# Turning the attention output of a fifth batch by transposing DMA instead of on TensorE, in a kernel whose instruction order is planned

## The chip, the cores and the metric

The kernel runs on one core of one Trainium2 chip. The metric is the device time of one execution in microseconds (us), the median of several runs. Ratios are computed as the mean time of one kernel's fast runs over the mean of the other's fast runs of the same rounds, so a ratio is not quite the ratio of the medians that stand beside it.

## The reference

The program is linear attention with exponential features, followed by a mixture of eight experts whose routing is normalised eight times over rows and columns (the gate, `P`). Shapes: 8 batches, 8 heads, 576 tokens, 64 channels; the experts see 4608 tokens of 512 features.

```python
def phi(x):
    proj = np.einsum('bhsd,df->bhsf', x, w_phi)
    proj = proj - np.max(np.abs(proj), axis=-1, keepdims=True)
    return np.concatenate([np.exp(proj), np.exp(-proj)], axis=-1)
q_p, k_p = (phi(q), phi(k))
kv  = np.einsum('bhsf,bhsd->bhfd', k_p, v);  z = np.sum(k_p, axis=2)
num = np.einsum('bhsf,bhfd->bhsd', q_p, kv)
den = np.einsum('bhsf,bhf->bhs', q_p, z)[..., None] + 1e-06
attn_out = num / den
# ... rows of attn_out, [4608, 512], are x of the experts:
for e in range(E):
    out += P[:, e:e + 1] * (np.maximum(x @ w1[e], 0.0) @ w2[e])
```

## The kernel before

The kernel is a Python program that collects all operations of the attention part and of the first expert with estimated durations, lets a list scheduler put them in order (`schedule`), and then emits them in that order. Each engine and each DMA queue is given its instructions in order.

```python
    def run(self, tc):
        done = self.schedule()          # sorted by the planner's own durations
        with tc.manual_schedule():
            for o in done:
                o.fn()
```

Queries and keys are loaded by POOL (GpSimd) into a buffer `qk` of which there are two; one half batch (four heads) fills one. SP (SyncE) then turns the whole buffer, 512 KB, with one transposing DMA into `qkT`. SP also loads the values and turns the rest tokens (`rT`).

```python
    ring(a_in, [128, 2, 4, NJ * D], BF16, "qk", 2)
    ring(a_t, [128, 2, 8, 128], BF16, "qkT", 3)
# ...
        for x, src in ((1, k), (0, q)):                       # load_qk
            dma("POOL", nh << 17, 230, lambda x=x, src=src: nc.gpsimd.dma_start(
                out=t["qk"]()[:, x, o:o + nh], in_=src[b, hh:hh + nh, 0:SM]...
# ...
            dma("SP", 1 << 19, 148, lambda: nc.sync.dma_start_transpose(   # turn_qk
                out=t["T"]().rearrange("p a b c -> p (a b) c"),
                in_=t["qk"]().rearrange("p a b c -> p (a b c)")),
                [(t["qk"], *y) for y in rk], [(t["T"], *y) for y in rk])
```

The attention output of a batch (512 main tokens, four pairs of heads) must be turned into `xT`, features on the partitions, before the expert's first matmul can use it. Batches 3 to 6 are turned by DMA; batches 0, 1, 2 and 7 by four TensorE transposes into PSUM (the buffers that TensorE's results go to in this kernel) and a copy on DVE (VectorE) for each pair; ACT is ScalarE:

```python
    def pair_c(b, pr, xb):
        if b in (3, 4, 5, 6,):
            dma("SP", 1 << 17, 148, lambda: nc.sync.dma_start_transpose(
                out=xT[:, pr, b * SM:(b + 1) * SM].rearrange("p (a c) -> p a c", c=128),
                in_=xb()[:, 0:NJ].rearrange("p a b -> p (a b)")), [(xb, 0), (xb, 1)], [("xT", b, pr)])
            return
        pxt = new("P1")
        for j in range(NJ):
            pe(128, lambda j=j: nc.tensor.transpose(
                bf(pxt)[:, j * 128:j * 128 + 128], xb()[:, j, :], ident),
                [(xb, 0), (xb, 1), "ident"], [pxt])
        dve(270, lambda: nc.vector.tensor_copy(
            out=xT[:, pr, b * SM:(b + 1) * SM], in_=bf(pxt)[:, 0:512]),
            [pxt], [("xT", b, pr)])
```

The softmax here doesn't subtract the row's maximum and nothing guards it: scores larger than these inputs give would overflow.

## Time and profile before

| before | value |
|---|---|
| median of 3 runs | 1026.67 us (1026.66 to 1026.98) |
| span of the profiled run, granted clock | 1026.8 us, 0.999 (that execution took 1028.55 us) |
| attention part with the first expert's start | up to about 205 us |
| remaining experts | about 820 us, TensorE 99% busy |

The prediction shows the page's totals and the stretches of the attention part, and explains them. One more view matters later: TensorE, stretch by stretch. The columns are the stretch, its length, then for matmul, weight load, DVE, ACT and POOL the busy us with the number of instructions, then the granted TensorE clock (1.00 is full speed), the DMA share (the queues' shares added, so it can pass 1), and GB/s. In the kernel before:

```profile
core 0: us, PE busy (x) PEld busy (x) DVE busy (x) ACT busy (x) POOL busy (x), PEclk, DMA share, GB/s
75.00:100.00 25.00, 24.74 (x287) 16.68 (x289) 24.06 (x59) 23.70 (x61) 21.32 (x34) 1.00 1.23 189
100.00:125.00 25.00, 24.79 (x276) 16.27 (x279) 22.65 (x51) 24.27 (x61) 18.15 (x28) 1.00 1.25 168
```

TensorE is busy for 49.5 of 50 us at full clock. One caution: the profiled execution took 1028.55 us, more than any of the four timed beside the kernel after (1026.66 to 1027.51). It is late from the start: its second group of gate matmuls (`wgate`) begins at 73.81 us, against 71.3 to 71.9 us in eight of the traces below, of kernels with the same order up to there. So starting times of two traces are not compared as they stand below; I count from that gate or from a neighbouring instruction.

These are the POOL queue's operations around 99 us in the kernel before (start, duration, engine, line, operation; in brackets the idle time before it and what ended it):

```profile
98.84 0.81 POOL L501 DMA_DIRECT2D qk<-in_k_dram  x1 [0.32 <-issue]
99.64 0.76 POOL L501 DMA_DIRECT2D qk<-in_q_dram  x1
100.40 1.94 POOL L761 TENSOR_TENSOR v<-v_m,em 128x1024 bf16<-128x1024 f32 x1
```

### The profile page before, as it was taken

To read this page: it belongs to the slowest core of one execution; us is meant where nothing else is said; L and a number is where in the kernel's file an instruction comes from. 1 tells how busy PE (TensorE), PEld (TensorE's weight loads), DVE (VectorE), ACT (ScalarE), POOL (GpSimd) and SP (SyncE) were. 2 spreads that over 40 slices of the span, in tenths; PEclk is the share of its full clock that TensorE was granted. 3 is DMA by queue.
4 is the path that set the end of the run, shared out by engine and by line. 5 is a ranking of instruction groups with operands and counts; after the bars stand their busy time and mean duration, and the time that the engine had idled before them with its cause. 6 is when DMAs were issued, how large, how long until landed. Compare 5 with 4: busy or idle time off the path is not lost.

```text
span 1026.8 us, 24281 instructions
## 1 busy us (share of the span) xinstructions
PE 1008.1 (98%) x9469; PEld 837.9 (82%) x9504; DVE 823.5 (80%) x1600; ACT 703.9 (69%) x1530; POOL 458.5 (45%) x480
## 2 busy tenths in 40 slices
PE   7899999999999999999999999999999999999998
PEld 4666666645888888888888888888888888888886
DVE  7999989987888887787777877787778877787775
ACT  7999999834888766666666666666665666666663
POOL 5768664400334444444444434544444433444342
PEclk9999999999999999999999999999999999999999
DMA  9999978170232611161115211341116111614333
GB/s 235 192 197 179 177 137 130 37 154 19 85 104 85 124 42 42 47 129 43 48 46 112 54 43 42 75 102 42 42 46 131 42 42 43 130 36 125 133 124 124
DMA packets 112501, 96.03 MB, mean 94 GB/s; under 512 B 54145, under 2 KB 87041, under 8 KB 112385
## 3 DMA queue, kind: packets, MB, share of 16 engines
q1 hardware_dynamic: 80576, 70.55, 26.5%
q0 software_dynamic: 31648, 23.86, 16.6%
q8 instruction: 74, 1.21, 0.5%
q14 instruction: 43, 0.34, 0.1%
q10 hardware_dynamic: 160, 0.07, 0.0%
HBM read 94.98 MB, written 14.16 MB: 106 GB/s over the span
## 4 chain that ended last, share of the span: by engine, by line
PE 93%; ACT 2%; DVE 1%; DMA 1%; SPq 1%; issue 1%; POOL 0%; DVEq 0%; ACTq 0%
PE ps L1273 74%; PE ps L573 17%; PE ps L856 2%; DMA acc<-in_q_dram 1%; ACT q L569 1%; ACT k L569 0%; SPq L495 0%; ACT wx L569 0%; SPq L551 0%; PE ps L885 0%; DMA xd<-S 0%; DVE ps L864 0%; DVE hT L1305 0%; DVE m L565 0%; POOL wx L761 0%
## 5 line engine op out<-in xcount | busy, mean ns | idle before, releaser
L1428 POOL TENSOR_TENSOR acc<-acc,V 128x512 f32<-128x512 f32 x248 | 314.8, 1280 | 484.5 <-ACT V L1425 426.7
L1301 ACT COPY U<-ps 128x512 f32<-128x512 f32 x378 | 217.0, 586 | 166.2 <-PE ps L1273 150.9
L1305 DVE CUSTOM_DVE_ANT_0 hT<-ps,U 128x512 bf16<-128x512 f32 x378 | 254.6, 687 | 87.7 <-PE ps L1273 59.9
L1425 ACT ACTIVATE V<-ps,P 128x256 f32<-128x256 f32 x496 | 208.1, 473 | 90.7 <-PE ps L1273 82.1
L1413 DVE SCALAR_TENSOR_TENSOR acc<-ps,P,acc 128x256 f32<-128x256 f32 x372 | 159.1, 478 | 69.5 <-PE ps L1273 69.2
L1273 PEld LDWEIGHTS <-S 128*128 128x128 bf16 x1984 | 194.1, 98 | 22.6 <-issue 0.2
L1273 PEld LDWEIGHTS <-T 128*128 128x128 bf16 x1512 | 148.0, 98 | 17.2
L1273 PEld LDWEIGHTS <-hT 128*128 128x128 bf16 x1488 | 145.6, 98 | 16.8
L1273 PE MATMUL ps<-X,T 128*128 128x256 bf16 x1008 | 152.4, 273 | 0.0
L1273 PE MATMUL ps<-T,S 128*128 128x256 bf16 x1056 | 135.8, 273 | 0.0
L1273 PEld LDWEIGHTS <-wx 128*128 128x128 bf16 x1152 | 112.7, 98 | 13.6 <-issue 0.2
L1181 DVE TENSOR_TENSOR S<-hT 128x1024 bf16<-128x1024 bf16 x124 | 87.2, 712 | 10.1 <-ACT hT L1310 9.9
L1273 PEld LDWEIGHTS <-w 128*128 128x128 bf16 x864 | 84.5, 98 | 9.8
L1273 PE MATMUL ps<-xT,wx 128*128 128x256 bf16 x576 | 88.4, 273 | 0.1
L1273 PE MATMUL ps<-X,wx 128*128 128x256 bf16 x576 | 86.8, 273 | 0.0
L1310 ACT ACTIVATE hT<-ps 128x512 bf16<-128x512 f32 x126 | 73.2, 606 | 9.8 <-PE ps L1273 9.8
L1273 PE MATMUL ps<-wx,hT 128*128 128x256 bf16 x560 | 77.6, 273 | 0.0
L1273 PE MATMUL ps<-xT,T 128*128 128x256 bf16 x504 | 76.7, 273 | 0.0
L573 PE MATMUL ps<-xT,w 128*128 128x512 bf16 x270 | 70.5, 379 | 0.7
L573 PE MATMUL ps<-w,hT 128*128 128x512 bf16 x276 | 69.8, 379 | 0.7 <-ACT q L569 0.2
L1273 PE MATMUL ps<-T,hT 128*128 128x256 bf16 x496 | 69.2, 273 | 0.0
L1273 PE MATMUL ps<-xT,w 128*128 128x256 bf16 x432 | 66.5, 273 | 0.0
(129 smaller groups left out, 1426.5 us busy)
## 6 DMA issues: line engine op xcount, KB each, us to landing
X<-xd SPq DMA_DIRECT2D x126, 256.0 KB, 2.7
wx<-in_moe_w_dram POOLq DMA_DIRECT2D x8, 1024.0 KB, 12.4
v_m<-in_v_dram SPq DMA_DIRECT2D x15, 512.0 KB, 5.6
out_dram<-acc SPq DMA_DIRECT2D x14, 512.0 KB, 2.9
w<-in_moe_w_dram POOLq DMA_DIRECT2D x6, 1024.0 KB, 12.1
xd<-S SPq DMA_DIRECT2D x18, 256.0 KB, 2.1
qk<-in_k_dram POOLq DMA_DIRECT2D x12, 256.0 KB, 5.5
qk<-in_q_dram POOLq DMA_DIRECT2D x12, 256.0 KB, 6.4
```

The lines of the kernel that those rows point to most:

```text
L569: act(el, lambda: nc.scalar.activation(out=dst(), in_=src(), func=ACT.Exp, bias=0.0, scale=scale), r, w)
L573: nc.tensor.matmul(out_, lhsT=lhsT, rhs=rhs, start=start, stop=stop)
L856: pe(65, lambda j=j: nc.tensor.matmul(pn()[:, j * D1:j * D1 + D1], lhsT=s["T"][x]()[:, j % 2, 2 * h + j // 2, :] if j < 4 else r["T"][x]() ...
L1181: lambda: f.tensor_tensor(out=out_(), in0=x(), in1=y(), op=op), r, w, **kw)
L1273: pe(256, lambda i=i, k=k, z=z: nc.tensor.matmul(bank()[:, 256 * i:256 * i + 256], lhsT=lhs(k, i), rhs=rhs(k), start=first and z, stop=k = ...
L1301: act(512, lambda: nc.scalar.copy(out=u[fp][n]().rearrange("p a b -> p (a b)"), in_=x[fp]()), [x[fp]], [u[fp][n]])
L1305: dve(515, lambda: nc.vector._custom_dve(ADD_SAT, out=out_(fp, i, j), in0=bank[fp]().rearrange("p (a b) -> p a b", a=2), in1=u[fp][n](), s ...
L1310: act(512, lambda: nc.scalar.activation(out=out_(fp, i, j), in_=x[fp]().rearrange("p (a b) -> p a b", a=2), func=ACT.Relu, bias=0.0, scale ...
L1413: dve(320, lambda n=n, ts=ts: nc.vector.scalar_tensor_tensor(out=acc[g][:, ts, 256 * j:256 * j + 256], in0=bank()[:, 256 * n:256 * n + 256 ...
L1425: act(370, lambda n=n: nc.scalar.activation(out=u()[:, n, :], in_=bank()[:, 256 * n:256 * n + 256], func=ACT.Copy, bias=0.0, scale=P[:, 4 ...
L1428: pool(695, lambda: nc.gpsimd.tensor_tensor(out=acc[g][:, 2 * i:2 * i + 2, 256 * j:256 * j + 256], in0=acc[g][:, 2 * i:2 * i + 2, 256 * j: ...
```

## The change

The intent is to take batch 2 off TensorE, DVE and PSUM as well, so that five batches instead of four are turned by DMA. The list of steps is the same; the planner sorts anew.

```diff
     def pair_c(b, pr, xb):
-        if b in (3, 4, 5, 6,):
+        if b in (2, 3, 4, 5, 6,):
             dma("SP", 1 << 17, 148, lambda: nc.sync.dma_start_transpose(
```

## The prediction

> **What bounds the kernel now.** I read the page first: busy time, and the chain that ended last.
>
> ```profile
> PE 1008.1 (98%) x9469; PEld 837.9 (82%) x9504; DVE 823.5 (80%) x1600; ACT 703.9 (69%) x1530; POOL 458.5 (45%) x480
> PE 93%; ACT 2%; DVE 1%; DMA 1%; SPq 1%; issue 1%; POOL 0%; DVEq 0%; ACTq 0%
> ```
>
> TensorE is the resource of the whole program, and 93% of the chain is TensorE work. The expert part (from about 205 us on) is not touched by the change; a microsecond won or lost before 205 us should reach the end unchanged. So the question is what the change does to the attention part. The view of stretches of time comes next (columns: stretch, length, busy us with instruction counts of matmul, weight load, DVE, ACT, POOL; granted clock; DMA share; GB/s).
>
> ```profile
> 30.00:75.00 45.00, 40.97 (x526) 29.22 (x530) 43.35 (x103) 43.45 (x107) 33.01 (x54) 1.00 1.18 182
> 75.00:205.00 130.00, 128.78 (x1493) 85.00 (x1513) 118.93 (x279) 122.78 (x301) 82.92 (x133) 1.00 0.87 134
> ```
>
> From 75 to 205 us TensorE shows 99%, ACT 94%, DVE 91%: three engines look full at once. But these busy times hold each instruction's latency, which overlaps with the next one's start. So I took start-to-start times from the timeline: a 128x512 exponential shows 0.67 us but seven in a row take 3.51 us, so one occupies (3.51 - 0.67)/6 = 0.47; a DVE maximum shows 0.68 but the next starts 0.60 later; eight 512-column matmuls take 1.89 us, so (1.89 - 0.38)/7 = 0.216 each; sixteen 65-column ones take 0.68, so 0.032 each. With the counts of the groups by form for the first 210 us:
> TensorE: 364 expert matmuls x 0.216 = 79, some 1150 of 65 columns x 0.032 = 37, 288 of 256 columns x 0.11 = 32, 72 projections of 512 columns x 0.216 = 16, everything else about 19; sum 183 us.
> ACT: 256 exponentials and 64 expert evictions x 0.47 = 150, 24 more of that size 11, 32 half-size 9, about 90 tiny ones 10; sum 180 us.
> DVE: 144 maxima x 0.60 = 86, 128 normalisations x 0.40 = 51, 64 reciprocals x 0.10 = 6, 32 kv copies x 0.34 = 11, copies into xT 10, the rest 12; sum 176 us.
> These are estimates from the trace, and they say the attention part is balanced: three engines with about 180 us of work each in 205 us, the difference being the start (inputs arriving) and many small waits. No single engine is a wall, so taking work from one buys less than that work.
>
> **What the Trainium skill says.** "Perfetto Trace Analysis", section Identifying the Most-Contended Engine, says that matmul busy share is a poor measure because pipelined matmuls mislead. The trace agrees: 99% busy, yet my count leaves some 10% of hidden gaps. "TensorE: Matmul & The Clock Gate", Part 4: PE-mode transpose: the result of such a transpose lands in PSUM, so a DVE copy must follow, and one takes about 275 ns in a kernel. Here one is 218 ns long and four together 0.39, and the copy does follow. "DMA: Bandwidth & Descriptors", section Latency and other measured facts, gives a transposing DMA 261 GB/s in its strided case: 128 KB would move in 0.50 us (an estimate from that figure). The trace shows much more from issue to landing, because of latency and queueing:
>
> ```profile
> L879 SPq DMA_TRANSPOSE xT<-xb x10: 1190/1194/1403, 96.0 to 189.9; - x10
> L879 SPq DMA_TRANSPOSE xT<-wx x6: 1189/1193/1935, 100.4 to 165.3; - x6
> DMA to landing us min/median/max: 2.3/4.2/7.7
> ```
>
> Those are the 16 turns of batches 3 to 6 that already go by DMA: 1.2 us of the SP queue each, 2.3 to 7.7 us to land. The same page, Rules for kernel authors, asks that transposes of two streams be serialized; all here are on the SP queue, so the change adds no such wait.
>
> **The change, part by part.** Batch 2 has four head pairs. The timeline shows their present turns: TensorE at 73.6, 78.5, 86.2 and 90.3 us.
>
> ```profile
> 86.24 0.39 PE L885 MATMUL ps<-ident,xb 128*128 128x128 bf16 x4
> 90.28 0.39 PE L885 MATMUL ps<-ident,xb 128*128 128x128 bf16 x4
> 88.19 0.39 DVE L888 COPY xT<-ps 128x512 bf16<-128x512 bf16 x1
> 91.01 0.42 DVE L888 COPY xT<-ps 128x512 bf16<-128x512 bf16 x1
> 96.31 1.89 PE L573 MATMUL ps<-xT,w 128*128 128x512 bf16 x8
> ```
>
> Removed: 16 TensorE transposes in groups of four. The next matmul starts 0.23 us after a group's start (73.58 to 73.81), so 4 x 0.23 = 0.9 us of TensorE. Removed too: four DVE copies of some 0.42, which hold DVE about 0.35 us (63.26 to 63.60), together 1.4 us. And four uses of a PSUM bank (of eight), each from transpose to end of copy: 1.0 us for the first (73.58 to 74.62), 2.3 us for the third (86.24 to 88.58). ACT loses nothing.
> Added: four 128 KB transposing DMAs, 4 x 1.2 = 4.8 us of the SP queue and perhaps 2 us of the DMA engines (4 x 0.5, estimate above).
> Moved: the Python planner sorts every instruction anew from its own durations, so the order on all engines shifts from about 73 us on, although the list of steps is the same. Nothing in the profile prices that.
> Is the DMA in time? The last pair's normalised output is ready at 89.56 us (89.08 + 0.48), and the first expert matmuls that use batch 2 (the 96.31 row; they follow the 64 of batches 0 and 1) reach that pair's part at about 97.0. That leaves 7.4 us for a turn with a median of 4.2 and a worst of 7.7, plus the time it queues on SP. The SP queue there:
>
> ```profile
> 84.84 1.36 SPq L518 DMA_TRANSPOSE qkT<-qk  x1
> 86.50 5.42 SPq L637 DMA_TRANSPOSE rT<-qk_r  x2
> 92.09 1.84 SPq L518 DMA_TRANSPOSE qkT<-qk  x1
> 94.06 1.00 SPq L509 DMA_DIRECT2D v_m<-in_v_dram  x1
> 95.97 1.20 SPq L879 DMA_TRANSPOSE xT<-xb  x1
> ```
>
> It is nearly solid from 84.8 to 97 us. The first two turns (ready at 73.3 and 78.0) find free places between 76 and 84 us; the last two either go ahead of the two rT turns and push everything behind by 2.4 us, or wait behind them. The data of the rT turns is first used at 103.5, so that is harmless; the query and key turn at 92.09 and the v load slip by 2.4 us, into the idle queue after 97.2.
> Sum if all is hidden: at most 0.9 (TensorE) to 1.4 (DVE) us. As ACT, just as full, is not relieved, I count half: -0.6 us. Against it I set +1.5 us for lost order: the step string and the set of batches look tuned together, and a re-sorted plan around a tuned one is more often worse. That 1.5 is judgement, some 1% of the 130 us after the change. 1026.7 - 0.6 + 1.5 = 1027.6 us.
>
> **The rivals.** (1) Clean gain: the turns hide and the freed slots on TensorE and DVE are used: 1025.3 to 1026.2. For it: both engines are nearly full in 75 to 205, and no wait of TensorE on a DMA of over 0.2 us lies between 70 and 130. Against: ACT. (2) DMA becomes the bound in this stretch: between 80 and 95 us the DMA share is 1.25 to 1.47 (the two queues overlap), so the turns or the loads behind them land late and TensorE starves: 3 to 6 us, 1030 to 1033. For it: landings up to 8.2 us for the query and key turns already. Against: each of those is issued many us ahead, and the planner fills a known delay with other work. (3) Only the order moves: gaps appear or vanish by a us or three with no relation to batch 2: 1024 to 1030. (4) The SP queue is in order, so a turn waiting for a late DVE result blocks the v and key loads behind it; this adds 1 to 3 us, 1028 to 1030.
>
> **Range and chances.** Rival 1 gives the lower end, 2 the upper: 1025.2 to 1031.5 holds them 8 times in 10. Two per cent is 20.5 us, a tenth of the attention part; the removed work is a twentieth of that, and to lose so much TensorE would have to stand still for several landings of the worst size. Faster by over 2%: 0.005; within 2%: 0.98; slower: 0.015.
>
> **What would show it.** Right: 16 fewer TensorE transposes (48 left) and four fewer DVE copies into xT (12 left), 20 DMA turns of xT, TensorE busy down by about 1 us or less, the expert part of the same length to 0.3 us, and the end of attention (last gate, now at 205.6 us) moved by the same amount as the total. ACT's work stays equal. Wrong: a wait of TensorE of over 1 us on an xT or qkT DMA between 90 and 105 us means rival 2; waits at SP's turns with late loads behind them, rival 4; a gain of over 1.5 us means that the banks or the new order gave more than the removed work; a difference in the expert part would contradict the first paragraph.

## More of the kernel before

POOL issues two loads of batch 5 into the second `qk` buffer and then scales the values of a half batch (`v`), which TensorE multiplies with the keys' features without a wait:

```profile
102.58 0.68 PE L573 MATMUL ps<-v,k 128*128 128x65 bf16 x16
```

Neither load waits for a turn here.

"Before" was run again beside every group of kernels, and each kernel is compared with the runs of before that it shared a chip with.

## The result and the profile after

| | before | after |
|---|---|---|
| median (range), 4 runs each, same chip | 1026.83 us (1026.66 to 1027.51) | 1036.38 us (1035.24 to 1037.79) |
| ratio of the means of the fast runs | | 1.0092 (95%: 1.0075 to 1.0110) |
| span of the profiled run, granted clock | 1026.8 us, 0.999 | 1035.6 us, 0.996 |
| start of the last gate's matmuls | 204.83 us | 213.54 us |

The change costs 9.5 us, about 0.9%: within 2%, but outside the predicted range. The last gate starts 8.7 us later and the span is 8.8 us longer, so all of it is lost in the attention part. (The trace of before is itself a slow execution, as said above; counted from the second gate to the last, before takes 131.02 us and after 141.86, 10.8 us more.) The page of the kernel after has 16 matmuls and four DVE instructions fewer, as predicted, but TensorE's busy time is up by 2.7 us (1010.8 against 1008.1), and there is a new entry, the query and key turn, in the chain that ended last:

```profile
PE 1010.8 (98%) x9453; PEld 838.4 (81%) x9488; DVE 822.9 (79%) x1596; ACT 704.6 (68%) x1530; POOL 459.0 (44%) x480
...
PE ps L1273 73%; PE ps L573 16%; PE ps L856 1%; DMA qkT<-qk 1%; DMA acc<-in_q_dram 1%; DVE m L565 1%; POOL v L761 0%; ACT q L569 0%; ACT k L569 0%; DVE ps L864 0%; DVE wx L565 0%; PE ps L703 0%; DVE xb L870 0%; DMA xd<-S 0%; ACT kr L569 0%
```

The stretches tell where. In the kernel after, first in 25 us, then two in 5 us (columns as above):

```profile
75.00:100.00 25.00, 22.20 (x244) 14.26 (x248) 21.23 (x51) 21.71 (x55) 18.88 (x30) 1.00 1.39 169
100.00:125.00 25.00, 19.76 (x187) 12.63 (x187) 16.26 (x37) 16.98 (x42) 13.94 (x21) 0.86 0.95 136
...
105.00:110.00 5.00, 3.15 (x51) 2.89 (x51) 1.82 (x5) 0.90 (x3) 4.64 (x6) 0.57 0.85 164
110.00:115.00 5.00, 4.78 (x35) 2.71 (x34) 4.07 (x10) 3.46 (x10) 0.42 (x3) 0.75 1.07 179
```

TensorE is busy 2.5 us less in the first stretch and 5.0 us less in the second, and in the second its clock is below full speed. The later stretches, 125 to 200 us, are nearly as full as before (73.9 of 75 us against 74.3). TensorE's timeline of the kernel after shows both standstills as bracketed waits:

```profile
97.16 1.24 PE L573 MATMUL ps<-xT,w 128*128 128x512 bf16 x5 [2.54 <-DMA xT<-xb]
...
106.85 1.04 PE L573 MATMUL ps<-v,k 128*128 128x65 bf16 x16 [4.96 <-POOL v L767]
```

The first is the wait for the last of the four new turns. The second, twice as long, is a wait for the scaled values from POOL, an operation that has nothing to do with batch 2. Why POOL was late is in POOL's own timeline of the kernel after:

```profile
103.86 0.80 POOL L501 DMA_DIRECT2D qk<-in_k_dram  x1 [6.28 <-DMA qkT<-qk]
104.69 1.92 POOL L761 TENSOR_TENSOR v<-v_m,em 128x1024 bf16<-128x1024 f32 x1
```

The load of the second half of batch 5 may not overwrite its `qk` buffer before the turn that reads that buffer has landed. POOL stands 6.28 us in front of that load, and the value product is behind it in the same queue. The turn in question is the sixth of the query and key turns (second half of batch 4); I call it **the sixth turn**. It is the one that the prediction showed at 92.09 us. The SP queue of the kernel after, where "x2" counts instructions of a group:

```profile
83.11 5.06 SPq L518 DMA_TRANSPOSE qkT<-qk  x1
88.26 1.51 SPq L879 DMA_TRANSPOSE xT<-xb  x1
89.95 3.10 SPq L637 DMA_TRANSPOSE rT<-qk_r  x2
93.16 1.21 SPq L879 DMA_TRANSPOSE xT<-xb  x1
94.97 3.33 SPq L518 DMA_TRANSPOSE qkT<-qk  x1
98.41 0.52 SPq L509 DMA_DIRECT2D v_m<-in_v_dram  x1
```

Two of the new turns (88.26 and 93.16) stand between the fifth query and key turn (83.11) and the sixth, and hold the queue for 1.51 + 1.21 = 2.7 us. The fifth turn itself holds it for 5.06 us, where it was 1.36 in before (84.84, shown in the prediction); the two `rT` turns hold it 2.3 us less. Counted from the start of the fifth turn, the sixth starts after 11.86 us, against 7.25 in before: it slips by 4.6 us. It also lands 8.3 us after its issue instead of 4.3, by the same view of the two traces. The chain of waits of the kernel after (start, duration, what) makes the link from there to TensorE:

```profile
93.16 1.82 DMA xT<-xb
94.97 8.33 DMA qkT<-qk
...
104.69 1.34 POOL v L761
...
106.85 1.04 PE ps L573 x16
```

**The sum.** Standstills: 2.5 + 5.0 us. Clock: the matmuls from 106.85 to 112.13 us, which last 5.28 us in the kernel after, take 2.92 us when the start-to-start times of the same groups are added up in the kernel before: 2.4 us. Together 9.9, of the 10.8 us by which the stretch from the second gate to the last grew. For the rest e2, described below, gives an estimate: with the new order and without any turn of batch 2 that stretch takes 132.75 us, 1.7 more than in before, of which 1.0 is a wait for POOL's product at the place of the 5.0; the other 0.7 makes the sum 10.6. The sum is an account of one trace against one trace. The Trainium skill, "TensorE: Matmul & The Clock Gate", Part 1: The HAM clock gate, says that TensorE's clock falls to half after an idle window of about 3.4 us and comes back after about as long a busy stretch. The trace agrees: after the standstill of 5 us the clock in 105 to 110 us is 0.57, and it is full again in 115 to 120 us. Other standstills here do not follow it (closing list).

This is a reading of a few traces. Whether the sixth turn is the cause, and what makes it late, was left to experiments.

### The profile page after: what moved, and what is told of

Read it like the earlier page. It is cut to its first block, busy times and chain, and to the rows that moved or that the text cites. A ratio compares the mean times of both kernels' runs of the same rounds, so it can differ in the third digit from the quotient of the medians.

```text
span 1035.6 us, 24246 instructions
## 1 busy us (share of the span) xinstructions
PE 1010.8 (98%) x9453; PEld 838.4 (81%) x9488; DVE 822.9 (79%) x1596; ACT 704.6 (68%) x1530; POOL 459.0 (44%) x480
## 3 DMA queue, kind: packets, MB, share of 16 engines
q8 instruction: 74, 1.21, 0.5%
HBM read 94.98 MB, written 14.16 MB: 105 GB/s over the span
## 4 chain that ended last, share of the span: by engine, by line
PE 92%; DVE 2%; DMA 2%; ACT 2%; issue 1%; POOL 1%; SPq 0%; DVEq 0%; POOLq 0%; ACTq 0%
PE ps L1273 73%; PE ps L573 16%; PE ps L856 1%; DMA qkT<-qk 1%; DMA acc<-in_q_dram 1%; DVE m L565 1%; POOL v L761 0%; ACT q L569 0%; ACT k L569 0%; DVE ps L864 0%; DVE wx L565 0%; PE ps L703 0%; DVE xb L870 0%; DMA xd<-S 0%; ACT kr L569 0%
```

## The experiments

My theory was that the added transposing DMAs take time of the SP queue, so that the sixth turn and the last new turn come late, and POOL's in-order queue hands the delay on to TensorE. The rivals were: the planner's new order alone costs the time; the bytes of the added DMAs cost it; TensorE's direct wait for the new turns' data costs it; the place of POOL's load in its queue is the weak point and moving it cures it. Line numbers differ by some 5 to 20 between the kernels, as lines were inserted. In the edits shown, `# ...` marks lines left out; assertions are left out too.

| kernel | this, median us (range) | before, same rounds | ratio (95%) |
|---|---|---|---|
| e1 old order, four DMA turns | 1036.77 (1035.56 to 1037.33) | 1026.40 | 1.0098 (1.0083 to 1.0113) |
| e2 new order, no turns | 1028.62 (1028.19 to 1029.07) | 1026.40 | 1.0021 (1.0004 to 1.0037) |
| e3 after, POOL load moved | 1034.31 (1033.20 to 1035.16) | 1026.40 | 1.0075 (1.0060 to 1.0090) |
| e4 old order, pairs 0 and 1 | 1029.07 (1026.09 to 1032.37) | 1026.40 | 1.0026 (1.0003 to 1.0049) |
| e5 old order, pairs 2 and 3 | 1032.95 (1029.78 to 1034.23) | 1027.21 | 1.0052 (1.0033 to 1.0071) |
| e6 before + four idle turns | 1035.87 (1031.85 to 1040.11) | 1027.21 | 1.0085 (1.0054 to 1.0116) |
| e7 before + four idle copies | 1028.11 (1027.08 to 1028.74) | 1027.21 | 1.0008 (0.9991 to 1.0024) |
| e8 before + four quarter turns | 1033.61 (1028.88 to 1035.59) | 1027.21 | 1.0056 (1.0027 to 1.0085) |
| e10 e6, loads held | 1031.60 (1030.97 to 1032.40) | 1026.91 | 1.0044 (1.0029 to 1.0059) |
| e11 after, loads held | 1039.02 (1037.40 to 1042.30) | 1026.91 | 1.0119 (1.0098 to 1.0141) |
| e12 before, loads earlier | 1026.74 (1026.06 to 1027.35) | 1026.91 | 0.9996 (0.9981 to 1.0011) |
| e13 e1, loads held | 1032.63 (1030.15 to 1037.87) | 1026.91 | 1.0070 (1.0040 to 1.0100) |
| e16 before, sixth turn late | 1037.11 (1036.54 to 1037.47) | 1026.21 | 1.0103 (1.0087 to 1.0120) |
| e17 e16, loads held | 1034.92 (1034.65 to 1035.84) | 1026.21 | 1.0083 (1.0067 to 1.0098) |
| e15 after, loads behind the product | 1036.04 (1033.41 to 1037.98) | 1026.21 | 1.0090 (1.0069 to 1.0111) |
| e9 batches 4 to 6 only | 1028.67 (1028.17 to 1029.59) | 1026.21 | 1.0021 (1.0006 to 1.0036) |

Four runs each of the kernels. e4, e6, e8 and e13 spread over 6 to 8 us from run to run, where before, in the rounds of the result, spreads over 0.9 us, and a trace shows one run: those of e4, e5, e6 and e11 are the slowest of their four, that of e13 is the fastest. So for these the trace tells which waits occur, and the table what they cost.

### e1 and e2: the turns without the new order, and the new order without the turns

e1 keeps the planner's input, and so the order of before, and puts a transposing DMA where the DVE copy of batch 2 was; the transposes are not emitted.

```diff
+        by_dma = b == 2 and pr in (0, 1, 2, 3)
         for j in range(NJ):
-            pe(128, lambda j=j: nc.tensor.transpose(
+            pe(128, (lambda: None) if by_dma else lambda j=j: nc.tensor.transpose(
# ...
-        dve(270, lambda: nc.vector.tensor_copy(
+        dve(270, (lambda: nc.sync.dma_start_transpose(
+            out=xT[:, pr, b * SM:(b + 1) * SM].rearrange("p (a c) -> p a c", c=128),
+            in_=xb()[:, 0:NJ].rearrange("p a b -> p (a b)"))) if by_dma else
+            lambda: nc.vector.tensor_copy(
```

> Planned exactly as the kernel before, so every engine keeps its old order; only the 16 transposes and 4 copies of batch 2 are left out and a transposing DMA is issued on the SP queue where each copy stood. Theory (late DMAs: the turns on a full SP queue land late, and hold up the query and key turns and, through them, the in-order POOL queue): still slower than before by 2 to 8 us, with a wait of TensorE on the xT DMA near 97 us and a wait of a POOL load on the qkT turn near 99 us. Rival (the re-sorted order is what costs): 1026 us or a little less, since the old order is kept and TensorE has 0.9 us less to do.

e2 keeps the order of after and emits nothing for batch 2's turns; that part of `xT` is set to zero at the start. Its result is wrong (relative error 0.35).

```diff
-            dma("SP", 1 << 17, 148, lambda: nc.sync.dma_start_transpose(
+            dma("SP", 1 << 17, 148, (lambda: None) if b == 2 else lambda: nc.sync.dma_start_transpose(
# ...
+                      nc.vector.memset(xT[:, :, 2 * SM:3 * SM], 0.0)), w=["wphi2"])
```

> Planned exactly as the kernel after, but the four turns of batch 2 are not issued at all; the batch 2 part of xT is set to zero at the start (wrong result on purpose). Theory (late DMAs): the loss is gone, 1024 to 1028 us, POOL waits less than 2 us for the qkT turns. Rival (re-sorted order): stays at 1033 to 1037 us, as every engine has the order of the kernel after.

Measured: the turns in the old order cost 10.4 us, the new order without them 2.2 us. The two don't add up to the 9.5 us of the change, and need not, as one wait can hide another. The order is not the cause: the four DMAs without it cost all of the time, and without the DMAs the new order costs 2 us (expected were 1024 to 1028). In e1 the biggest wait of TensorE is another one than in after, though. Its timeline has

```profile
103.86 2.29 PE L573 MATMUL ps<-xT,w 128*128 128x512 bf16 x5 [8.19 <-DMA xT<-xb]
```

because there the last new turn stands behind the sixth turn in the SP queue (issued at 96.87 after 94.21), while POOL waits 6.40 us on the sixth turn too. Two waits lie side by side, and the longer one sets the time.

### e4 and e5: two pairs at a time

Both are e1 with fewer pairs.

```diff
-        by_dma = b == 2 and pr in (0, 1, 2, 3)     # e1
+        by_dma = b == 2 and pr in (0, 1)           # e4;  (2, 3) in e5
```

> As the first run of this call, but only pairs 0 and 1 of batch 2 go by DMA (their turns fall at 74 and 78 us, where the SP queue has free places); pairs 2 and 3 stay on TensorE. Theory (late DMAs on a full SP queue): 1025.5 to 1027.5 us, no new wait. Rival (any additional transposing DMA in a stretch in which the DMA engines are full costs): slower than before by 1 to 4 us.

> The old order, pairs 2 and 3 of batch 2 by DMA, pairs 0 and 1 on TensorE. Theory: most of the loss of all four is here, since these two fall among the four large turns of 84 to 94 us and the last one is needed 7 us after it is ready: 1031 to 1036 us, with a wait of TensorE of over 3 us on an xT DMA. Rival (loss grows with the number of turns, wherever they are): about as slow as pairs 0 and 1, 1028 to 1030 us.

Measured: 2.7 us for the first two pairs and 5.7 us for the last two, 8.4 together against 10.4 for all four. e4 missed its expectation of no new wait: TensorE waits 2.38 us for POOL's value product (in its slowest run; its fastest, 1026.09, lost nothing). No added turn stands between the fifth and the sixth turn there, yet the sixth starts 9.46 us after the fifth (93.81 against 84.35), 2.2 later than in before. What has changed is the fifth turn:

```profile
84.35 5.29 SPq L518 DMA_TRANSPOSE qkT<-qk  x1
```

It holds the queue for 4.05 to 5.53 us in all eleven kernels with two DMAs added some 3 to 13 us ahead of it, plain copies too, and for 1.35 to 1.36 in the seven others, e5 among them; the two `rT` turns behind it then take 2.5 to 3.8 us instead of 5.4 to 6.3. Why is not known. In e5 the sixth turn is as late (91.75, 9.47 us after the fifth), but it lands in 4.3 us, as in before, where e4's takes 6.1; POOL doesn't wait, and TensorE waits 5.00 us for the data of the last new turn. So there are two ways to lose: the sixth turn lands too late for POOL, or the last new turn lands too late for TensorE.

### e6, e7 and e8: what of a DMA costs, when nobody waits for its data

These keep before whole and add DMAs behind batch 2's DVE copies, into the part of `xT` of batch 7, which is written properly much later. Nobody reads what they write.

```diff
+        def copy():
+            nc.vector.tensor_copy(out=xT[:, pr, b * SM:(b + 1) * SM], in_=bf(pxt)[:, 0:512])
+            if b == 2:
+                nc.sync.dma_start_transpose(                        # e6: four turns of 128 KB
+                out=xT[:, pr, 7 * SM:8 * SM].rearrange("p (a c) -> p a c", c=128),
+                in_=xb()[:, 0:NJ].rearrange("p a b -> p (a b)"))
# e7: nc.sync.dma_start(out=... the same ..., in_=xb()[:, 0:NJ]), four plain copies of 128 KB
# e8: nc.sync.dma_start_transpose(out=xT[:, pr, 7 * SM:7 * SM + 128], in_=xb()[:, 0]), four turns of 32 KB
```

> The kernel before with its order and all its TensorE turns of batch 2, plus four more transposing DMAs of 128 KB at the same four places of the SP queue; they write a part of xT that is overwritten much later, so nothing waits for their result. Theory (the additional turns delay the other DMAs: the qkT turns land later, the POOL loads that wait for them block the v product, and TensorE stands): slower than before by 3 to 7 us although no one needs the added data; the wait of a POOL load on a qkT turn of 2.5 us or more shows. Rival (the loss is the direct wait of TensorE on the late xT turns, 8.2 us in the first run): 1026 to 1027.5 us.

> The same as the run with four idle turns, but the four additional DMAs are plain copies of the same 128 KB from SBUF to SBUF. If what costs is the bytes on the full DMA engines, as slow as the idle turns within 1.5 us. If it is the transposing (a turn holds the SP queue or the engines longer than its bytes), at least 2 us faster than with the idle turns, 1026 to 1028 us.

> The same as the run with four idle turns, but each turn moves a quarter, 32 KB. If the cost is DMA engine time in proportion to the size, a quarter of the loss of the idle turns, up to 1.5 us over before; if it is a fixed price of each issue on the SP queue, about the whole loss.

Measured: idle turns cost 8.7 us, quarter turns 6.4 us, and plain copies of as many bytes as the full turns 0.9 us, which isn't told from nothing (the interval holds 1). So neither the bytes nor the wait for the data explains the loss; of the DMAs added, only the transposing ones made it. The SP queue shows one difference between them. In e7 and e8, the third of the four:

```profile
91.14 0.51 SPq L892 DMA_DIRECT2D xT<-xb  x1
```

```profile
92.32 1.15 SPq L892 DMA_TRANSPOSE xT<-xb  x1
```

A plain copy holds the queue 0.48 to 0.58 us, a turn 1.12 to 1.23 even with a quarter of the bytes. In e7 the sixth turn starts at 91.82, lands in 4.6 us, and POOL waits 0.56 us; in e8 it starts at 93.65 and lands in 10.3 us. Counted from the fifth turn's start, that is 7.54 and 9.43 us, 1.9 us apart: 0.6 by the longer hold of the added turn (1.15 against 0.51), and 1.2 by that of the fifth turn (5.29 against 4.05). POOL's timeline of e8 has the same picture as after's, and the value product follows at 106.06:

```profile
104.50 0.81 POOL L501 DMA_DIRECT2D qk<-in_k_dram  x1 [8.27 <-DMA qkT<-qk]
```

The Trainium skill, "DMA: Bandwidth & Descriptors", Issuing engines are not separate DMA queues, says two things that bear on this: that the time to initiate a DMA on its engine is usually small relative to the DMA itself, and that DMAs of all issuing engines run on the same 16 DMA engines and interleave. On the first e8 agrees: a turn's issue took 1.12 to 1.23 us, its landing 5.2 in the median. Yet four of them cost 6.4 us, so a small issue time is no small cost where the queue is full. That the time in the queue, and not the work in the DMA engines, is the price is argued, not tested apart; what speaks for it is that from 0 to 205 us the packets of the hardware queue, SP's, take 57.9% of the DMA engines' time in e8 and 59.2% in e7 (57.2% in before). On the second see e10 to e17.

### e16: the sixth turn late, and nothing else

The sharpest test adds no DMA at all. It is before with the sixth turn moved two places later in the SP queue, behind the v load and one turn of `xT`, which move up in exchange.

```diff
     def run(self, tc):
         done = self.schedule()
+        turn = self.turns[5]
+        at = done.index(turn)
+        to = [i for i in range(at + 1, len(done)) if done[i].eng == "SP"][1]
+        done.insert(to, done.pop(at))
# ... turns: a list to which turn_qk appends each whole turn
```

> The kernel before, nothing added; the sixth qkT turn stands two places later on the SP queue, behind the v load and the first xT turn of batch 3, so it starts near 97 us instead of 92, after the POOL loads of 95.5. Theory (race): it lands in 8 to 11 us instead of 4.3, a POOL load waits 5 us or more for it, TensorE waits for the v product, and the time is 1030 to 1036 us without a single added transfer. Rival (it takes added turns): it lands in 4 to 6 us and the time stays under 1029 us.

Measured: +10.9 us, with the same instructions as before. The turn starts at 96.41 and lands in 8.1 us. POOL's and then TensorE's timeline of e16:

```profile
105.06 0.81 POOL L507 DMA_DIRECT2D qk<-in_k_dram  x1 [7.48 <-DMA qkT<-qk]
```

```profile
108.79 1.04 PE L580 MATMUL ps<-v,k 128*128 128x65 bf16 x16 [7.04 <-POOL v L774]
```

Counted from the fifth turn, the sixth starts after 11.76 us, against 7.25 in before and 11.86 in after. A sixth turn that is 4.5 us late is enough to lose as much as the change does, through the chain that the trace of after shows. This settles the main point: the slip of this one turn, which the prediction called harmless, costs. It doesn't show that the slip is all that costs in after: there TensorE also waits for the last new turn, and e5 loses 5.7 us by that wait with its sixth turn landed in time.

### e3 and e15: the load taken out of the product's way

If the value product suffers only because a waiting load stands ahead of it in POOL's queue, moving that load should help. e3 is after with the k load of batch 5's second half moved behind the next product and its cast; e15 moves all four loads of batch 5 behind the product.

```diff
# e3, on after
+        at = done.index(self.later)               # the k load of batch 5, heads 4 to 7
+        to = [i for i in range(at + 1, len(done)) if done[i].eng == "POOL"][1]
+        done.insert(to, done.pop(at))
# e15, on after; held: the four q and k loads of batch 5, stop: the last non-DMA POOL
# operation ahead of the last of them
+        for o in self.held:
+            done.remove(o)
+        at = done.index(stop) + 1
+        done[at:at] = self.held
```

> The kernel after with one change on POOL: the load of k for the second half of batch 5, which waits 6.3 us for the landing of a qkT turn, is issued after the v product that stands behind it, instead of ahead. Theory (the POOL queue is blocked by that load, and TensorE waits 5.0 us for the v product and then runs at a cold clock): 5 to 8 us faster than after, 1028 to 1031 us, and no clock dip at 105 to 115 us; the 2.5 us wait on the xT DMA stays. Rival (DMA bandwidth is simply short, the block on POOL is only where it shows): the wait reappears elsewhere and the time stays within 2 us of after, 1034 to 1037 us.

> The kernel after, with all four POOL loads of batch 5 (q and k, both halves) behind the v product of that place, so that no v product stands behind a load that waits for the sixth qkT turn. Theory: the 5.0 us wait of TensorE for the v product and most of the cold clock go; the wait on the late xT turn (2 us) and the late key and query data stay: 1029 to 1032 us. Rival (the DMA engines are simply overloaded): 1034 us or more, TensorE then waiting for other late data.

Measured: 7.9 us over before for e3 and 9.8 for e15, against 9.5 for the change; both missed their theory (1028 to 1031 and 1029 to 1032 us), and the rivals' ranges hold them. The 5 us wait is gone from both traces, and the time is hardly better. In e3 POOL then waits 3.27 us on the same turn one operation later, and TensorE 2.91 us at 106.52 for an ACT result. In e15 TensorE's timeline shows two standstills in other places:

```profile
98.26 2.29 PE L586 MATMUL ps<-xT,w 128*128 128x512 bf16 x5 [2.63 <-DMA xT<-xb]
...
124.68 1.01 PE L586 MATMUL ps<-wphi,qkT 128*128 128x256 bf16 x6 [2.73 <-ACT wx L582]
125.48 3.42 PE L586 MATMUL ps<-w,hT 128*128 128x512 bf16 x8
```

The first is after's wait for the last new turn. The second goes back to POOL again: at 118.05 a k load had waited 3.05 us for a result of TensorE, and a product and a scaling were behind it, for which ACT waited 2.90 us. Each standstill is followed by slow matmuls: the five at 98.26 take 0.42 us each from start to start, where after's five at 97.16 take 0.21. From 75 to 125 us TensorE is busy 5.4 us less than in before, and the clock of 0.96, 0.97 and 0.93 in three stretches of 25 us stands for another 3.5 us (25 x 0.14), an estimate that together makes 8.9; from the second gate to the last, e15 takes 9.8 us longer than before (140.85 against 131.02). So the load in front of the product is the way by which the delay of the turn came to TensorE in after, but not the only way: once the loads are late, the delay comes by the next one. The rival, that moving the load cures it, falls.

### e10, e11, e12, e13 and e17: does the turn land late because it meets loads?

In after the sixth turn starts 4.6 us late and takes 4.0 us longer to land. If transfers of both queues interleave, as the page cited under e8 says, the theory follows: in before the turn has a lead over POOL's loads of batch 5's first half (92.09 against 95.49) and runs mostly alone; in after it starts when the k load at 93.30 is already in flight. e10, e11, e13 and e17 are e6, after, e1 and e16 with these two loads held back by three POOL operations; e12 is before with them earlier.

```diff
# e10 on e6, e11 on after, e13 on e1, e17 on e16; held: the k and q loads of batch 5, heads 0 to 3
+        last = max(done.index(o) for o in self.held)
+        to = [i for i in range(last + 1, len(done)) if done[i].eng == "POOL"][2]
+        stop = done[to]
+        for o in self.held:
+            done.remove(o)
+        at = done.index(stop) + 1
+        done[at:at] = self.held
# e12 on before: the same two loads put ahead of the second POOL operation before them
+        to = [i for i in range(first) if done[i].eng == "POOL"][-2]
```

> The run with four idle turns (1035.9 us), and the two POOL loads of q and k for the first half of batch 5 issued three POOL instructions later. In the runs so far the second large qkT turn of this stretch lands in 4.3 to 4.6 us where it is issued 1.5 us or more ahead of these loads, in 6.1 at 0.8 to 1.0 ahead, and in 8.2 to 10.3 level with them or behind. Theory (a race: additional turns make this turn late on the SP queue, so that it meets the loads in the DMA engines): with the loads held back the turn lands in 4 to 5.5 us although the four turns are still there, the POOL wait on it falls below 3 us, and the time to 1027 to 1030 us. Rival (the number of turns itself slows everything, the loads don't matter): the turn still takes over 7 us and the time stays above 1033 us.

> The kernel after with the same two loads held back. Theory: the turn of 95 us lands in 4 to 5.5 us instead of 8.3, the 5.0 us wait of TensorE for the v product and the cold clock that follows are gone, and the xT wait shrinks to 1 us or so: 1027 to 1030 us. Rival: over 1033 us.

> The kernel before, without any added turn, but the same two loads issued ahead of the v product that stood before them on POOL, so some 2 us earlier, about 1 us after the qkT turn starts instead of 3.4. Theory: the turn lands in 6 us or more instead of 4.3, the POOL load behind it waits 1 to 3 us, and TensorE loses 1 to 5 us: 1028 to 1032 us. Rival (it takes the additional turns): 1026 to 1027.5 us.

> The first run (old order, all four turns by DMA, 1036.8 us), with the two loads held back. Theory: the last xT turn, which stands behind the qkT turn on the SP queue and landed 8.2 us late, lands 3 to 5 us earlier, since the turn ahead of it is not slowed: 1029 to 1033 us. If it reached 1026 the change would pay nothing and cost nothing.

> As the run with the late turn, and the two loads of the first half of batch 5 three POOL instructions later, at about 98.5 us. Theory: with 1.3 us or so of lead the equally late turn lands in 4.3 to 6.5 us, the POOL wait is 3 to 5 us shorter than in that run, and the time at least 2 us less. Rival: no difference over 1 us.

What the traces show of the sixth turn in the kernels, with its lead over the first of these loads (negative where the load was first):

| kernel | turn starts | load starts | lead | lands after |
|---|---|---|---|---|
| before | 92.09 | 95.49 | 3.4 | 4.3 us |
| e9 | 90.20 | 93.54 | 3.3 | 4.3 us |
| e15 | 97.72 | 103.35 | 5.6 | 4.6 us |
| e13 | 93.03 | 96.63 | 3.6 | 4.8 us |
| e10 | 94.75 | 96.53 | 1.8 | 5.4 us |
| e5 | 91.75 | 93.41 | 1.7 | 4.3 us |
| e7 | 91.82 | 93.34 | 1.5 | 4.6 us |
| e17 | 94.98 | 96.40 | 1.4 | 7.6 us |
| e12 | 89.59 | 90.95 | 1.4 | 4.3 us |
| e2 | 90.44 | 91.45 | 1.0 | 6.1 us |
| e4 | 93.81 | 94.63 | 0.8 | 6.1 us |
| e1 | 94.21 | 94.31 | 0.1 | 8.2 us |
| e11 | 97.73 | 97.52 | -0.2 | 11.0 us |
| e8 | 93.65 | 93.19 | -0.5 | 10.3 us |
| e6 | 98.13 | 97.52 | -0.6 | 10.3 us |
| e3 | 94.64 | 93.88 | -0.8 | 8.7 us |
| after | 94.97 | 93.30 | -1.7 | 8.3 us |
| e16 | 96.41 | 94.55 | -1.9 | 8.1 us |

No run shows the interleaving itself, only the landings. With a lead of 1.4 us or more the turn lands in 4.3 to 5.4 us, with 0.8 to 1.0 in 6.1, with less in 8.1 to 11.0, in all kernels but e17. In time, holding the loads went both ways. e10 is 4.7 us above before where e6 was 8.7, and e13 5.7 where e1 was 10.4; in e13's trace, its fastest run, POOL's wait no longer reaches TensorE, which keeps one wait of 3.44 us, on the last new turn. In e10 the turn is about as late as in e6 (9.62 us after the fifth turn's start, against 9.97) and lands in 5.4 us instead of 10.3, so there the gain goes with the lead; the time, 1031.6, still misses the 1027 to 1030 expected. e11 was a miss: it is worse than after (12.1 us above before); in its trace the sixth turn slid to 97.73, and the held load stood just ahead of it all the same. e12 did what it was to do, and its theory failed: the lead fell from 3.4 to 1.4 us, the landing stayed at 4.3, and the time didn't change (-0.2 us). e17 has the same lead of 1.4 us, yet its turn takes 7.6 us, and the kernel is only 2.2 us better than e16. So the lead is not the whole cause. In e17 (as in e16) the v load of 512 KB was issued ahead of the turn, at 91.38; it may be the traffic that the turn met there. That is argued, not tested.

### e9: one batch fewer

If turns by DMA are dear in this queue, fewer of them might be better than before.

```diff
-        if b in (3, 4, 5, 6,):
+        if b in (4, 5, 6,):
```

> Replanned with only batches 4, 5 and 6 by DMA; batch 3, whose turns fall at 96 to 114 us, goes back to TensorE. Theory: four fewer turns in a stretch where they cost, against 0.9 us of TensorE and 1.4 us of DVE more: 1024 to 1028 us, the re-sorted order being worth 2 us either way (the run without any turns of batch 2 was 1.6 to 2.2 us slower than before). Rival (turns are worth what they relieve): 1028 us or more.

Measured: 2.5 us slower than before. Whether turning batch 3 on TensorE is what costs isn't shown: the planner sorted anew here too, and in e2 a new order alone was 2.2 us. No version tried is told apart from before on the faster side.

## Why the prediction was wrong

**What held.** There are 16 fewer matmul records and four fewer DVE instructions, 20 DMA turns of `xT`, ACT's work is equal, and the last gate moved by 8.7 us with the span's 8.8: the expert part is untouched. TensorE's busy time did not fall as said; it rose by 2.7 us, as matmuls at half clock are busy for longer (the sixteen behind the 5 us standstill 1.04 us, in before 0.68). "+1.5 us for lost order" was about right: e2 measures 2.2 us for the new order without the turns, which also holds whatever the planner gains by it. That this came out near is partly luck: the prediction called it judgement. Two of the signs that the prediction named for its rivals appeared: a wait of TensorE of over 1 us on an `xT` DMA between 90 and 105 us (2.54 us), and late loads behind the turns in the SP queue (the v load comes 15.3 us after the fifth turn's start, in before 9.2).

**The step that failed.** The prediction wrote: "The data of the rT turns is first used at 103.5, so that is harmless; the query and key turn at 92.09 and the v load slip by 2.4 us, into the idle queue after 97.2." The slip was foreseen, at 2.4 us; counted from the fifth turn it was 4.6, as the fifth turn too held the queue longer (5.06 us against 1.36). With it falls the step before, that the first two turns "find free places": e4, with these two alone, made the sixth turn 2.2 us late. But the mistake that matters is "harmless". For the `rT` turns the prediction asked when their *output* is first used, for the sixth turn only whether the queue has room. The turn also *frees* a buffer: there are two `qk` buffers, and POOL's next k load waits for the turn to have read one of them. That load stood at 98.84 in before, 2.4 us after the turn had landed (92.09 + 4.3 = 96.4). So the slack was 2.4 us, and behind the load in the same queue was a product that TensorE needed at 102.58. A slip of 4.6 and a landing 4.0 longer, less 2.4 of slack, leave 6.2 us; POOL waited 6.28. e16 shows that such a slip, with nothing added, costs 10.9 us.

**The landing.** The prediction took the landing times of before as they were. The sixth turn's went from 4.3 to 8.3 us when it slipped, nearly as much again as the slip. A lead over POOL's loads goes with it in 17 of 18 kernels; e17 is the exception, and e12 with the same lead of 1.4 us lands in 4.3, so what doubles it stays open.

**The wait on the new turns' own data.** The prediction left 7.4 us for a last turn with a median landing of 4.2 and counted it as hidden. The last new turn was issued at 93.16 behind the two `rT` turns, and TensorE waited 2.54 us for it. e5 and e1, where it was 5.00 and 8.19 us, show that this is a loss in its own right when the turn falls behind the sixth.

**The rivals' sizes.** Rival 4 was the right mechanism in part ("The SP queue is in order"), but it saw the block in the loads behind the turn on SP, where the costly one was POOL's; it was sized at 1 to 3 us, and rival 2 at 3 to 6. Neither counted the half clock after a long standstill (2.4 us here), nor that two standstills add up. The loss in the trace is made of 2.5 + 5.0 + 2.4 us and some 0.7 of new order.

**The balance of the engines.** The prediction set 99% busy, which is 75 to 205 us, against a count of 183 us, which is the first 210, start included (196 us busy by the profile), and found some 10% of hidden gaps and no wall. Redone with its own times for 75 to 205 us alone, the count is about 125 of 130 us (an estimate): some 4% of gaps. TensorE is close to a wall there, so little of a standstill can be made up.

**Copies against turns.** The prediction priced a turn at 1.2 us of the SP queue; e8 shows 1.12 to 1.23, the trace after 1.21 to 1.60. It had no price for what the turns do to the fifth turn's hold. Copies with half the issue time and the same bytes cost 0.9 us, which is not told from nothing.

## What to carry to other kernels

When an added instruction delays another in an in-order queue, don't ask only when the delayed one's result is first read; ask also which buffer it sets free, which load waits for that buffer, and what stands behind that load in its own queue. A delay of 4.5 us in a DMA queue came out as 10.9 us in e16, as it picked up a longer landing and, after the standstill, a slower TensorE clock. To test a suspect, delay it alone in the kernel before, with nothing added: if that gives a loss of the size in question, the suspect is enough for it. The rest of the change isn't acquitted by that; e5 shows a second way to lose. And before two traces are subtracted, check that each is a typical run, and count from a common point.

## What the Trainium skill lacked or had wrong

- "DMA: Bandwidth & Descriptors" gives a transposing DMA as a bandwidth and, in its part on trn3, as sequencer cycles of earlier chips for other shapes; no page gives the time for which such a turn holds the issuing queue here: 1.12 to 1.23 us per turn of 32 KB (e8), 1.2 us in the median per turn of 128 KB (before), against 0.48 to 0.58 us for a plain copy of 128 KB (e7). Four turns of 32 KB cost the program 6.4 us, four copies of 128 KB 0.9 us.
- No page gives the landing of a transposing DMA beside loads of the other queue ("DMA: Bandwidth & Descriptors" would be the place). One turn of 512 KB landed in 4.3 us with the loads issued 3.4 us behind it and in 8 to 11 us with them issued at the same time or ahead; one run (e17) doesn't fit.
- The same turn's issue itself took 1.84 us in before, 3.33 in after and 5.66 in e16: the time for which a large turn holds its queue isn't fixed, and no page gives the spread. The fifth turn's was 1.35 to 1.36 us, or 4.05 to 5.53 where two small DMAs had been issued ahead of it.
- "TensorE: Matmul & The Clock Gate" ties the fall to half clock to an idle window of about 3.4 us. In e15 it followed standstills of 2.63 and 2.73 us (0.42 and 0.41 us per 512-column matmul right after them), while after's standstill of 2.54 us left the clock full (0.21), and so did e13's of 3.44 us (clock 1.00 in 95 to 110 us).
